# Two transfers instead of six for the gathered heads, weight loads tied to units, and a new order of the first region

## The chip, the cores and the metric

The program runs on one core of one Trainium2 chip, all in float32. The metric is the device time of one execution in microseconds (us). A run's time is that of the whole execution; a profiled execution also has a span, which is the part between its first and last recorded instruction.

## What is computed

Three layers follow each other: a gated linear attention with complex decays, a soft mixture of experts over all tokens, and a mixture that routes each token to one expert. Cut to what matters:

```python
def _attn_ref(q, k, v, a_re, a_im):          # 4 batches, 8 heads, 768 steps, 48 features
    mag = np.sqrt(a_re * a_re + a_im * a_im)
    scale = np.minimum(mag, 0.999) / (mag + 1e-06)
    a_re_n, a_im_n = (a_re * scale, a_im * scale)
    for t in range(S):
        new_re = ar * S_re - ai * S_im       # ar, ai: step t, one value per feature d
        new_im = ar * S_im + ai * S_re
        S_re, S_im = (new_re + k_t v_t^T, new_im)
        y[:, :, t] = q_t^T S_re

def _moe_ref(x, phi, w1, w2):                # x: 3072 x 384, 8 experts, 32 slots
    logits = x @ phi
    slot_input = softmax(logits over tokens).T @ x
    slot_out[e] = relu(slot_input[e] @ w1[e]) @ w2[e]      # 384 x 1024, 1024 x 384
    return softmax(logits over slots) @ slot_out

def _moe2_ref(x, w_gate, w1, w2):            # each token goes to its best of 8 experts
    out[mask] = gate_w * (relu(x[mask] @ w1[e]) @ w2[e])
```

## The kernel before

**Units and groups.** The attention's 3072 tokens are cut into 24 units of 128 steps (4 batches of 6 chunks). One unit holds all 8 heads. Units are taken in 13 groups of one or two; a group's decays `a_re`, `a_im` are loaded together (`decl_A`, L415) and turned into logarithms and angles. For each unit, `decl_B` (L442) loads k, q and v, forms running sums of the logarithms and of the angles with TensorE (L457, a product with a triangular matrix) and multiplies k and q by the exponentials (L466, L467). `decl_C` (L494) makes the features and does the unit's attention.

**Features and the gathered heads.** The features lie on the partitions: tile `F` (L349) has three blocks of 128 partitions. Heads are taken in four pairs. A block holds the 48 features of one head of its pair at partitions 0 to 47 and of the other at 64 to 111. The fourth pair has no block of its own: a third of each of its heads (16 features) sits in the spare partitions 48 to 63 and 112 to 127 of each block. `feature_rows` (L45) lays this out on the host. L505 multiplies k and q by cosine and sine into `F` (VectorE, or GpSimd where the order says so). Then the thirds of the fourth pair have to be brought together: for each of its two heads, three DMAs on SyncE's queue (L509) each move 16 partitions of one block into tile `M`, 16 x 513 floats or 32.1 KB each, six DMAs a unit:

```python
for i in range(2):
    for j in range(3):
        d, o = 64 * i + 16 * j, 64 * i + 48
        dma(32768, lambda j=j, d=d, o=o: nc.sync.dma_start(out=M[d:d + 16, :nx], in_=F[o:o + 16, j, :nx]), ...)
```

**The unit's products.** TensorE transposes the k features (L528; copied to `kT` by L532 and L533, whose second copy puts the gathered pair's features into the same order as `M`), multiplies q features by k features to scores (L543, three head pairs from `F` and the fourth from `M`), forms the k-v products (L563), the part of the output inside the chunk (L581) and the part from the carried state `S` (L590, again with `F` and `M`), and transposes the output (L618). VectorE masks the scores (L552) and updates the state (L605, L607, L609). Every fourth unit, `decl_M` (L628) adds the four units to the soft mixture's logits and to a running softmax over tokens. After the last unit a short closing chain ends with `siT` (L673), the slots' inputs.

**The second region** begins with the soft mixture's experts: first layer L797 with the `w1` weights of 8 experts (four products of 12 matrix steps), transposes L806, second layer L826 with the `w2` weights (four products of 16 steps), then L837 and the routed layer.

**Weights.** Each expert's `w1` and each `w2` is 1536 KB. Eight tiles `wr0` to `wr7` lie beside the first region's tiles and take the eight `w1` (L728). Five tiles `wl0` to `wl4` take the place of the first region's tiles (features, k and q, v, ...) once these are done, and hold `w2` of experts 0 to 4 (L774). The `w2` of experts 5 to 7 go into `wr0` to `wr2` after the first four first-layer weights are used, in halves of 768 KB (L814). All transfers named here are issued by SyncE and stand in its one queue in the order of the program.

**What sets the order.** `Sched.op` (L127) records each operation with its engine, an estimated duration and what it reads and writes. For the first region a table of numbers, `ORDER[0]`, gives a sequence of all operations and which engine does those that have a choice; it is followed word for word (`follow`, L210). `place` (L147) walks that sequence with the estimated durations, `MODE` (L102, the cost of changing from one kind of matrix product to another) and `LAT`; `emit` (L222) writes the instructions in the order of the start times so found. So every engine executes its own fixed list, in order, and the semaphores make it wait where an input is not there. `emit` also puts small unused products (`fill`, L731) into TensorE's gaps near the start. In the sequence of before, five of the eight `w1` loads stand among the units and three after or around the last unit's gather.

Of the kernel before, what the change touches and what calls it, by code (L numbers as in the profile page):

```python
# [44 lines left out]
def feature_rows():  # L45

    f = np.zeros((3, 128), np.int64)
    for j in range(3):
# [21 lines left out]
    "FaQ()7yvW?JODrdH~>WeNB|H3TmVb}U;tzQBme*aPykc_tN^e8v;b%Ui~t+}EC5&lXaH>hZ~zPdkN}hbm;i_Xpa3WUxB#R8r~sS*y#RCocmTuzgaC{I%mBauI2FkN1OY$++yHz4kO7nd>;Uxu_yEKK"  # L70
    "nE{{y1ORLS<N$yG2mwR^odNs+&;ZB*00AHX@BrWd%mHu#r~%Od*#SraOaXKOd;!z|tO3{nv;oxtumN}hfB_f*3<13X-~ojJxB*ZB>;mWk+yUhQ906nj@B)Yd00I;OI0IAx5CIec^Z^J05dsVX^aAJr"
    ">;Y{8ECC<_JOd;G9Rm0P@Bx?t7y=*xBmw*ZC;>156a&BkX##)(SOFLV`2sWnGy*sRcmkmUKm+^&Z~`a-I00M%U;!`!d;**Tqyj7ga037XR0BN$gaSkZNdt5P1Or$DTmyIm90MQ&r~-5XX#*$&tO6th"
    "1OhPw2m@>bd;^37JOWSxOao8@hysBFKmtSpNCHd(U;~H)umZFKR05;{%mfSrECav-!~)0yWCP3s&;m3DGy{<Xj02PdoC93~paYBo5Ci-KqyzK>m;<Z>SOSm&NClJvv;#~9PzAUGxdTlEyaLb!00pQ6"
    "NCeaZWCUCUzyrhs)C5=r+ycA<$O9Aw-~t#0*#sN~R0J#qcmz-c+ypoV%mdg01O*WV2nFB+<O6{OYy=DiU<4!u&;!&1R0VtlgaqIOFa_iU*aL_Jj08Le_yqg|AO)NRumdy|+ym$X>;sSl00bxnbp$vC"
    "lms*dK?UdpJO%IrKnC;!pafV2qy%6E_yg<&Tm|q1Xa%SQtOT$G2n1yX<N|O6cm==&zy-Vo=mKO0Xa-ycYzBY@1q4I|fChvHa0P4y>;?1%@dXS7L<SKA6a+m4d<B>Uc?O&YXatA`7zA(zbOn?KyadDq"
    "NCq4Ppawt$&;`i^bOwwDkOs5_xCXoiqz14CgawEN*ag4_%mw%btOg(i)CG(Mlm+|+$OXg(SOzQv;04SExCCSfkOj~Ns0PRe<ORe9U<OPE=>>cSXb9W|00syKlm{^c1O^xg)CQObm<E^yoCTl-wFaaG"
    "s0G{x6b4WRR0c!{7zTI<qz4=bum_w6*#_tatOaZcL<9^55C*UX90p(lWCA1vAPB4n2nWOm5eI+>BnAuzoCqKWC<cTGj0pS&NC=1sxCaFX<OTo-a0qk=pa@I|Bnb2dC<sspqzEVnya&Mt>;^0cL<h(R"
# [1331 lines left out]
```

## Time and profile before

| what | value |
|---|---|
| median of 3 runs | 320.6 us (319.21 to 322.67) |
| the profiled execution, its own time | 322.03 us |
| its span | 320.0 us |
| mean granted TensorE clock, as a share of full speed | 0.947 |
| TensorE matmul busy | 278.9 us, 87% of the span |
| VectorE busy | 230.3 us, 72% |
| ScalarE busy | 202.1 us, 63% |
| GpSimd busy | 80.1 us, 25% |
| moved by DMA | 62.79 MB, mean 196 GB/s |

The first region ends, and L797 begins, at 235.7 us of the span; the second layer L826 ends at 273.2 us. A matmul's record in float32 counts twice (two passes), so "x16" in a row of TensorE is eight matrix steps. Busy time is an average over stages with different limits, so the stages are read one by one. Idle time of an engine that nobody waits for costs nothing.

### The profile page before, as it was taken

The page shows a single profiled execution, that of the slowest core. Times are in us where ns is not written, and L with a number is a line of the kernel's source. Part 1 is how long each engine was busy: PE and PEld are TensorE (multiplying, and loading weights), DVE is VectorE, ACT ScalarE, POOL GpSimd, SP SyncE. Part 2 cuts the span into 40 slices and gives each one's busy share as a digit, 9 for nine tenths or more (in the row PEclk, how much of TensorE's full clock was granted, in tenths as well). Part 3 has the DMA queues.
Part 4 walks back from the last instruction along what each step waited for, and adds up shares of the span by engine and source line. Part 5 has one row for each costly group of instructions (what it writes and reads, how often), then busy time and mean ns, then how long its engine had stood idle before and what let it go on. Part 6 is the DMA issues. An engine that isn't in the chain of part 4 may idle for free.

```text
span 320.0 us, 9381 instructions
## 1 busy us (share of the span) xinstructions
PE 278.9 (87%) x3764; PEld 220.0 (69%) x3764; DVE 230.3 (72%) x478; ACT 202.1 (63%) x423; POOL 80.1 (25%) x94
## 2 busy tenths in 40 slices
PE   0995989889999998998899898979898597999990
PEld 0884868769878877887778697867642132688970
DVE  2689898799989999986989886866465030558750
ACT  7599598968998898997597766543232010434760
POOL 1016225534433557340452324111000000000000
PEclk9998799999999999997999999999979798967997
DMA  7934366564656345548275535554899993190482
GB/s 243 349 80 147 109 205 190 160 228 140 189 170 193 113 147 165 189 115 311 74 247 188 174 83 169 176 183 141 340 378 373 374 371 136 48 349 1 186 325 88
DMA packets 32323, 62.79 MB, mean 196 GB/s; under 512 B 4128, under 2 KB 19872, under 8 KB 32272
## 3 DMA queue, kind: packets, MB, share of 16 engines
q1 hardware_dynamic: 32272, 62.12, 58.3%
q8 instruction: 31, 0.51, 0.7%
q14 instruction: 20, 0.16, 0.2%
HBM read 52.66 MB, written 4.72 MB: 179 GB/s over the span
## 4 chain that ended last, share of the span: by engine, by line
PE 46%; DVE 11%; DMA 9%; SPq 9%; issue 3%; ACT 1%; DVEq 0%; ACTq 0%
PE bank L543 6%; PE bank L581 5%; PE bank L457 5%; SPq L509 5%; DMA M<-F 5%; PE bank L590 4%; DMA wr<-w 4%; SPq L814 3%; DVE F L505 3%; PE bank L797 3%; PE bank L563 3%; PE bank L528 2%; PE bank L618 2%; PE bank L1121 1%; PE bank L826 1%
## 5 line engine op out<-in xcount | busy, mean ns | idle before, releaser
L457 PE MATMUL bank<-cst,lt 128*128 128x128 f32 x288 | 41.3, 287 | 9.4 <-DMA cst<-cst 8.3
L457 PEld LDWEIGHTS bank<-cst,lt 128*128 128x128 f32 x288 | 36.4, 197 | 11.8 <-ACT lt L435 8.3
L505 DVE TENSOR_TENSOR F<-kqi,lt 128x768 f32<-128x768 f32 x35 | 39.7, 1158 | 3.7 <-PE bank L590 2.7
L543 PE MATMUL bank<-F 48*128 48x128 f32 x576 | 41.1, 284 | 0.4 <-DVE kqi L466 0.3
L543 PEld LDWEIGHTS bank<-F 48*128 48x128 f32 x576 | 36.4, 192 | 5.0 <-issue 1.6
L552 DVE TENSOR_TENSOR sc<-bank,cst 128x512 f32<-128x512 f32 x48 | 31.3, 684 | 10.4 <-PE bank L543 9.9
L733 ACT ACT_TABLE_LOAD x27 | 34.6, 1283 | 1.2 <-PEq L1392 0.7
L581 PE MATMUL bank<-sc,v 128*64 128x128 f32 x384 | 31.9, 292 | 2.6 <-DMA v<-v 1.8
L505 POOL TENSOR_TENSOR F<-kqi,lt 128x768 f32<-128x768 f32 x13 | 24.9, 1925 | 29.2 <-PE bank L590 14.5
L479 POOL TENSOR_TENSOR lt<-lt,n 128x384 f32<-128x384 f32 x15 | 16.7, 1115 | 45.2 <-DVE n L478 39.9
L581 PEld LDWEIGHTS bank<-sc,v 128*64 128x64 f32 x384 | 21.6, 143 | 8.1 <-issue 4.5
L543 PE MATMUL bank<-M 48*128 48x128 f32 x192 | 18.8, 284 | 8.6 <-DMA M<-F 7.2
L590 PE MATMUL bank<-F,St 48*48 48x128 f32 x480 | 25.6, 283 | 0.0
L411 ACT COPY yT<-bank 112x256 f32<-112x256 f32 x39 | 13.6, 373 | 16.4 <-PE bank L590 14.0
L528 PE MATMUL bank<-cst,F 128*128 128x128 f32 x120 | 20.1, 286 | 3.9 <-DVE F L505 2.9
L543 PEld LDWEIGHTS bank<-M 48*128 48x128 f32 x192 | 15.3, 188 | 10.8 <-issue 7.4
L411 ACT COPY kT<-bank 128x288 f32<-128x288 f32 (+1 forms) x63 | 18.6, 328 | 5.8 <-PE bank L528 3.9
L590 PEld LDWEIGHTS bank<-F,St 48*48 48x48 f32 x480 | 16.2, 122 | 6.1 <-issue 5.4
L826 PE MATMUL bank<-wl,hT 128*32 128x384 f32 x80 | 16.0, 601 | 4.3 <-DMA wl<-w 4.3
L563 PE MATMUL bank<-v,kT 128*48 128x48 f32 x640 | 19.7, 210 | 0.0
L563 PEld LDWEIGHTS bank<-v,kT 128*48 128x48 f32 x640 | 17.1, 125 | 3.6 <-issue 2.1
L528 PEld LDWEIGHTS bank<-cst,F 128*128 128x128 f32 x120 | 13.9, 145 | 6.1 <-DVE F L505 2.2
(249 smaller groups left out, 594.7 us busy)
## 6 DMA issues: line engine op xcount, KB each, us to landing
wr<-w SPq DMA_DIRECT2D x8, 1536.0 KB, 8.5
kqi<-kq SPq DMA_DIRECT2D x24, 384.0 KB, 3.6
reim<-reim SPq DMA_DIRECT2D x11, 768.0 KB, 5.2
wl<-w SPq DMA_DIRECT2D x5, 1536.0 KB, 17.2
v<-v SPq DMA_DIRECT2D x24, 192.0 KB, 3.5
wr<-w SPq DMA_DIRECT2D x6, 768.0 KB, 12.2
M<-F SPq DMA_DIRECT2D x120, 32.1 KB, 2.4
out<-osb SPq DMA_DIRECT2D x10, 384.0 KB, 2.4
```

What stands on the lines that cost most here:

```text
L411: v = {"A": ("ACT", t_act(n, True), lambda: nc.scalar.copy(out=out, in_=in_()), False), "D": ("DVE", t_dve(n), lambda: vec.tensor_copy(out ...
L457: pe.matmul(bank(kb)[:, 128 * i:128 * i + 128], lt[:, j, 128 * i:128 * i + 128], (tri, tri2)[j], start=True, stop=True)
L479: either("P", 384, lambda e: e.tensor_tensor(out=lt[:, 1], in0=lt[:, 1], in1=n, op=ALU.subtract), r=[kth, kn], w=[kth])
L505: either(e, 768, lambda e, i=i, b=b: e.tensor_tensor(out=Fv[:, i], in0=kq, in1=b, op=ALU.mult), r=[(kkq, 0), (kkq, 1), klt(u, i)], w=[kF[i]])
L528: pe.transpose(bank(kb)[:, 128 * j:128 * j + 128], F[:, j, 128 * x:128 * x + 128], idn)
L543: pe.matmul(bank(kbs[i])[:, 128 * q:128 * q + 128], kind(q, i, x), kind(q, i, 2 + x), start=(x == 0), stop=(x == 1))
L552: op("DVE", t_dve(512), lambda i=i, msk=msk: vec.tensor_tensor(out=sct[scs[i]], in0=bank(kbs[i]).rearrange("p (h t) -> p h t", h=4), in1=m ...
L563: pe.matmul(kvps[64 * i:64 * i + 48, q, 48 * x:48 * x + 48], w, v[:, 48 * h:48 * h + 48], start=True, stop=True)
L581: pe.matmul(out(q, i, 64), v[:, 48 * h:48 * h + 64], sct[scs[i]][:, q], start=True, stop=(c == 0))
L590: pe.matmul(out(q, i, 48), S[64 * i:64 * i + 48, q, 48 * x:48 * x + 48], kind(q, i, 2 + x), start=False, stop=(x == 1))
L733: tab = lambda t: nc.scalar.preload_act_table_set(TABLES[t])
L826: pe.matmul(bank(kbo)[32 * j:32 * j + 32, :384], hT[2 * q + hf][:, k, 32 * j:32 * j + 32], w2v(4 * q + j)[:, 4 * hf + k], start=(hf == 0 a ...
```

## The change

It has four parts.

1. `feature_rows` gives block j every third feature of the gathered heads (j, j+3, j+6, ...) instead of 16 features in a row. So the three blocks' values of one partition are three features in a row, and one DMA moves a whole head: 16 partitions x 3 blocks of `F` go to 48 partitions of `M`. A unit has two gathers of 96 KB instead of six of 32 KB. `kT`'s second copy writes in the new order.
2. The eight `w1` loads are declared beside units 4, 6, ..., 18, and an empty TensorE operation of units 6, 8, ..., 20 is said to read them, so that a sequence has to place each load before that point. The operation issues nothing, so no engine waits for these loads there.
3. The planner's estimates are changed: a gather is 620 + 2100 ns, a change of product kind always 97 ns, and the products' durations are new.
4. `ORDER[0]` is a new sequence for the first region, with other choices of engine.

```diff
@@ feature_rows
-            f[j, 64 * i + 48:64 * i + 64] = 48 * pair(3)[i] + 16 * j + np.arange(16)
+            f[j, 64 * i + 48:64 * i + 64] = 48 * pair(3)[i] + j + 3 * np.arange(16)
@@ ORDER
...
-MODE = [[0 if i == j else 95 if j else 24 for j in range(5)] for i in range(5)]
-for _i, _j in ((1, 2), (2, 1), (1, 3), (3, 1), (2, 3), (3, 2), (1, 4), (4, 1), (2, 4), (4, 2), (3, 4), (4, 3)):
-    MODE[_i][_j] = 95
+MODE = [[0 if i == j else 97 for j in range(5)] for i in range(5)]
@@ decl_C
         for i in range(2):
-            for j in range(3):
-                d, o = 64 * i + 16 * j, 64 * i + 48
-                dma(32768, lambda j=j, d=d, o=o: nc.sync.dma_start(out=M[d:d + 16, :nx], in_=F[o:o + 16, j, :nx]), r=kF + kX, w=[("M", u % NF, i, j)])
+            d, o = 64 * i, 64 * i + 48
+            op("SP", 620, lambda d=d, o=o: nc.sync.dma_start(out=M[d:d + 48, :nx], in_=F[o:o + 16, :, :nx]), r=kF + kX, w=[("M", u % NF, i)], lat=2100)
...
-                copy("D", 96, kTt[b][:, 288:].rearrange("p (i j r) -> p j i r", j=3, i=2), lambda kv4=kv4: kv4()[:, :, :, 48:], r=[kb], w=[("kT", b, 1)])
+                copy("D", 96, kTt[b][:, 288:].rearrange("p (i r j) -> p j i r", j=3, i=2), lambda kv4=kv4: kv4()[:, :, :, 48:], r=[kb], w=[("kT", b, 1)])
...
-        op("PE", 2, lambda: None, r=kF, w=[kbs[0]], acq=kbs[0], mode=2)
-        op("PE", 870, SC((0, 1)), r=kF, w=kbs, acq=kbs[1], mode=2)
-        op("PE", 870, SC((2, 3)), r=kF + kM, w=kbs, mode=2)
+        kwt = [("w", u // 2 - 3)] if 6 <= u < 6 + 2 * NWR and u % 2 == 0 else []
+        op("PE", 2, lambda: None, r=kF + kwt, w=[kbs[0]], acq=kbs[0], mode=2)
+        op("PE", 893, SC((0, 1)), r=kF, w=kbs, acq=kbs[1], mode=2)
+        op("PE", 893, SC((2, 3)), r=kF + kM, w=kbs, mode=2)
...
@@ the loop over groups
         for u in us:
             decl_B(u)
+            if u % 2 == 0 and 4 <= u < 4 + 2 * NWR:
+                i = u // 2 - 2
+                dma(1572864, lambda i=i: load_w(wr[i], *w_src[i]), w=[("w", i)])
...
-    for i in range(NWR):
-        dma(1572864, lambda i=i: load_w(wr[i], *w_src[i]), w=[("w", i)])
```

What the new sequence does is seen in the lists of the engines. The first place is SyncE's queue at the end of the first region. `M` from `F` is a gather, `wr` from `w1` a first-layer weight load, `wl` from `w2` a second-layer load. Before:

```order
L448 DMA kqi1_105<-kq 128x768
L449 DMA v3_109<-v 128x384
L389 DMA wr4_81<-w1 128x3x1024
L509 DMA M1_113<-F1_111 16x512 x6
L389 DMA wr6_83<-w1 128x3x1024
L389 DMA wr1_78<-w1 128x3x1024
L389 DMA wl0_2912<-w2 128x8x384
L389 DMA wl1_2913<-w2 128x8x384
```

The same place in the changed kernel (its lines are three lower):

```order
L505 DMA M0_112<-F0_110 48x1x513 x2
L445 DMA kqi1_105<-kq 128x768
L505 DMA M1_113<-F1_111 48x1x512 x2
L446 DMA v3_109<-v 128x384
L386 DMA wl0_2825<-w2 128x8x384
L386 DMA wl1_2826<-w2 128x8x384
```

The three `w1` loads around the last gather are gone from here; `wl0` follows the last unit's gathers and its v. The eighth `w1` load now stands before the gathers of the third unit from the end.

The second place is SyncE's queue in the middle of the first region, around a `w1` load. `reim` is a group's decays, `kqi` and `v` the inputs of one unit. Before:

```order
L449 DMA v0_106<-v 128x384
L389 DMA wr0_77<-w1 128x3x1024
L428 DMA reim1_97<-reim 128x2x768
L509 DMA M1_113<-F1_111 16x513 x6
L509 DMA M0_112<-F0_110 16x513 x2
```

And in the changed kernel, around another such load:

```order
L386 DMA wr5_82<-w1 128x3x1024
L425 DMA reim0_98<-reim 128x2x768
L445 DMA kqi1_105<-kq 128x768
L446 DMA v1_107<-v 128x384
L505 DMA M1_113<-F1_111 48x1x513 x2
L505 DMA M0_112<-F0_110 48x1x513 x2
L445 DMA kqi0_104<-kq 128x768
```

One load more stands before the first units' inputs, at the start of the program, and six stand among the units, mostly with a `reim` load right behind.

The third place is TensorE's list from the last unit's output to the last product that makes `siT`. The names are: `x` with `dd` the softmax-weighted tokens, `yT` with `phiI` the last unit's logits, `ex` and `ltc` transposes of exponentials and logits, `stw` with `acc` and `dd` with `x_129` the sums that make `siT`. Before:

```order
L681 MATMUL bank_75<-x_126,dd 32x384
L681 MATMUL bank_75<-x_127,dd 32x384
L681 MATMUL bank_75<-x_128,dd 32x384
L700 MATMUL bank_74<-cst,row 128x1
L637 MATMUL bank_71<-yT_124,phiI 128x128 x4
L690 MATMUL bank_70<-cst,ltc 128x128
L618 MATMUL bank_72<-cst,yT_124 128x112 x4
L706 MATMUL bank_74<-mx,cst 128x1
L690 MATMUL bank_69<-cst,ltc 128x96
L665 MATMUL bank_71<-cst,ex 128x32
L662 MATMUL bank_73<-stw,acc 128x32 x3
L670 MATMUL bank_73<-dd,x_129 128x32 x3
```

And in the changed kernel:

```order
L615 MATMUL bank_72<-cst,yT_121 128x112 x4
L634 MATMUL bank_74<-yT_124,phiI 128x128 x4
L678 MATMUL bank_75<-x_126,dd 32x384
L678 MATMUL bank_75<-x_127,dd 32x384
L678 MATMUL bank_75<-x_128,dd 32x384
L703 MATMUL bank_69<-mx,cst 128x1
L662 MATMUL bank_74<-cst,ex 128x32
L687 MATMUL bank_73<-cst,ltc 128x96
L615 MATMUL bank_70<-cst,yT_124 128x112 x4
L687 MATMUL bank_74<-cst,ltc 128x32
L659 MATMUL bank_71<-stw,acc 128x32 x3
L667 MATMUL bank_71<-dd,x_129 128x32 x3
```

The last unit's logits now stand ahead of the weighted-token products instead of behind them; the number of products up to `siT` is nearly the same.

Counted over the whole first region in the two lists: TensorE changes from one kind of product to another 142 times before and 133 times now. VectorE makes 33 of the 48 feature products instead of 35 (GpSimd 15 instead of 13) and 10 of the 20 subtractions of L479 instead of 5. ScalarE has two more table loads. The table of numbers itself is not shown.

## Rows read from the trace of the kernel before

**Rows 1.** The profile's page: busy time, and the DMA share in 40 slices.

```profile
PE 278.9 (87%) x3764; PEld 220.0 (69%) x3764; DVE 230.3 (72%) x478; ACT 202.1 (63%) x423; POOL 80.1 (25%) x94
...
DMA  7934366564656345548275535554899993190482
```

**Rows 2.** Stretches: from:to, length, busy of each engine, granted clock, DMA share, GB/s.

```profile
20.00:230.00 210.00, 192.97 (x3153) 162.95 (x3154) 178.71 (x343) 160.12 (x340) 77.86 (x80) 0.98 0.55 172
...
235.00:247.00 12.00, 11.78 (x87) 3.58 (x86) 7.91 (x12) 3.56 (x6) 0.00 (x0) 0.87 1.06 373
247.00:269.00 22.00, 16.07 (x132) 5.39 (x136) 3.06 (x8) 1.09 (x4) 0.00 (x0) 0.92 0.96 337
...
273.20:320.00 46.80, 37.76 (x262) 32.75 (x260) 26.79 (x80) 20.95 (x45) 0.64 (x1) 0.85 0.47 171
```

**Rows 3.** The chain that ended last, end of the second layer: start, length, what.

```profile
235.67 6.56 PE bank L797 x48
...
256.92 11.79 DMA wr<-w
268.75 4.47 PE bank L826 x28
```

**Rows 4.** Timeline of TensorE, first and second layer: start, length, instruction, [idle before].

```profile
242.16 0.66 PE L806 MATMUL bank<-cst,hid 128*128 128x128 f32 x4
242.75 2.78 PE L797 MATMUL bank<-wr,siT 128*32 128x512 f32 x24
...
251.98 4.36 PE L826 MATMUL bank<-wl,hT 128*32 128x384 f32 x26 [3.39 <-DMA wl<-w]
...
259.45 2.76 PE L826 MATMUL bank<-wl,hT 128*32 128x384 f32 x32
```

**Rows 5.** Timeline of SyncE's queue, 212 to 244 us: start, length of the issue.

```profile
212.33 0.43 SPq L389 DMA_DIRECT2D wr<-w  x1
218.50 3.71 SPq L509 DMA_DIRECT2D M<-F  x6
222.25 2.10 SPq L389 DMA_DIRECT2D wr<-w  x2
224.45 19.51 SPq L389 DMA_DIRECT2D wl<-w  x5
```

**Rows 6.** What TensorE waited for, 20 to 235 us: total us, times, longest.

```profile
PE bank L543 <- DMA M<-F: 7.2, 7, 2.2
PE bank L528 <- DVE F L505: 2.9, 3, 1.2
```

**Rows 7.** The gather's line L509: issue in ns (least, median, most); landing.

```profile
L509 SPq DMA_DIRECT2D M<-F x144: 507/587/1973, 19.4 to 221.6; - x144
...
DMA to landing us min/median/max: 1.9/2.3/5.5
```

**Rows 8.** DMA issues: count, KB each, median us to landing.

```profile
v<-v SPq DMA_DIRECT2D x24, 192.0 KB, 3.5
...
reim<-reim SPq DMA_DIRECT2D x2, 192.0 KB, 2.5
```

**Rows 9.** The chain in the middle: one and two runs of the same product.

```profile
95.00 0.58 PE bank L590 x16
...
96.96 1.02 PE bank L590 x32
```

**Rows 10.** Timeline of TensorE at the first unit's gather, columns as in rows 4.

```profile
27.24 0.81 PE L543 MATMUL bank<-M 48*128 48x128 f32 x8 [2.21 <-DMA M<-F]
```

**Rows 11.** One stretch of 6 us behind that, columns as in rows 2.

```profile
30.00:36.00 6.00, 5.12 (x32) 3.94 (x33) 6.00 (x8) 3.96 (x8) 2.04 (x2) 0.50 0.12 27
```

**Rows 12.** Costly groups of the page that the change moves.

```profile
L505 DVE TENSOR_TENSOR F<-kqi,lt 128x768 f32<-128x768 f32 x35 | 39.7, 1158 | 3.7 <-PE bank L590 2.7
...
L733 ACT ACT_TABLE_LOAD x27 | 34.6, 1283 | 1.2 <-PEq L1392 0.7
```

**Rows 13.** Copies into kT by engine and shape, ns.

```profile
L411 ACT COPY kT<-bank x63: 217/387/424, 20.6 to 217.9; 128x288 f32<-128x288 f32 x34, 128x96 f32<-128x96 f32 x29
```

More of the change, by code (lines that the diff above doesn't have):

```diff
@@ L69 @@
 ORDER = [
[L70 to L77, printed above, removed]
@@ new lines @@
+    "Gy&`Yv;p7%U;#J*i2;lOxB)!@ya7M~WC3UazyWXplmVCl^Z=XzQ~}Tc_yGI>00F!L8~}9z1OW&GTmftWcmc=(kO9R33<KBz%mEMq)dA1}*Z~j&6ay3i7y&>7^Z}#+-~pfk00Kk-Bmt-aAOWobNC5}|"
+    "3<3B7Ndim){Q*n?zyeSK83V)uumLCmL<8sn>;c>X1Of;GTmta{EdlHT$O0q-AOr9M<O1{p903#pU;<?V3<CH9=mJOsC<815OamAK5CSj)%mQ=*cmg>C0RtQZFasO{AOhq8Py+k{R0C83d;-t{SOPQx"
+    "XaZ3KI0!rgSOX*iC;}`3fC5|tgaVKP1OtEsGy{|Zm;#&v-~ylm)B<G#`~+wNa03wp*aB?=tOBtDZ~}M(00o2ts03^SI0A?Qgam;Di~@}Vd;{D9%moYt6a=IKJpu#;$OPa7%mj!8jRY(Nhy&0Bv;w#S"
+    "<OHw;v;>d@xCD>`7z6|W)C9l;yaeb3qywk}*aVaVm;=NF2?aO=JOn@lbOV$Gm;}%TU;~^3paZM}r~<$PL<H0Y*affyv;(*UNCZ>_SOn|@oCGig3<VSg5Cyyg%meTQ!~<LeU<70Ypahf$9Rwf+^aRKQ"
@@ new lines @@
+    "`2-yW`~`FbGz35bqy!)Ya0Ji;00smGXay(*C<OEcB?Q$2WCcV57zQ*390uG4cm#a}gauFrm<Qkmcm*H^B?b`&6b4KLfCYR7C<agjhy{%W2nHktR0f;}*aPGRECnnEkOf!<Fa<OPYy~(5Kn7?8+yq<("
+    "pa<LoYy><8a0QeFm<4nNJO$_lqy_K=WCmddYzAlstOPIyI0YC5L<S57patv&Km|kvs09E7Nd}|`s0T;|Oa)K{Bng}aSOwq%B?sUK_yyz##0MA%xCM9y<O5U%tOc+Iv<1Kgyakj7od)m&bp`|k=m+%!"
+    "?FUT;Tm_g0hz5`bKnExZ2n3A=@CSef_yfoX%m-ivv<A2aNe4s+AO|!D90>daAPB4nd<HlNga*6^BnbQm*ay%CJO|JRpa!G{um`jUOb4h2C<m|xtOhIx)CVjH)CTki00=1va0XBZR0l8#U<bSgzy<^e"
+    "EC{FyFbKp3Tn7;dWCvIWXa{Tu$Og;?2naL@Gzb+4a0j>t3<z`wcn5q3pb6XtI0--q_y^bqga=#*U<il@JqS<;=mS^?R0zZc$pusiSP3u(un52hObMh3tO{ia-3L$!JPEW2;0CY?KnX|)gbC#aL<nFB"
@@ new lines @@
+    "Yzc4)bP2c!s0ru>6bD2JXb5ZwTnT6iWC`2|tO;-k>;`lQ;0U}3<Op~OObB=hd<lpNj0uDYkO`Ctd<cLDhzLjtfCsb+j0o@skO-6runD*cm<YfK><F|8&<N-Vpa`4@xC)pF#0bm^^a{lZr3mx}I1Km*"
+    "{0IOE*a*A|1PKTU_zL_A6bZozoCz2Q>;w1)j0eaG)CkQ8EDHe(L<&F(&<fZJ1P43}$p~NykOvqE1Pd?=5DUx+2nX;8+zQ|dGz&ls90$M(<O+ZZ^ayDR><TywKnn~B5DCNz&<Ows)Cpw@Yzh<$7z@}5"
+    "ND4g*ObT!cbPC`J{02k}+zAK^=nCWs=n3oz@CqCYNDN2|@Coz@{0YbkgbYLrcnS;)ybM(fR0>!MT?%{(ObciXhzyJjQ43HC01hAv3<vlL2nuWr5C?D!Obi4LBnyxXlnluW#0$U-hzbk}fC`KXkP4X!"
+    "5DF9u7z$tvgbI8NlnOKoC<|~4WDB4SbPUuAcnqiroC;73SPN(i019mj1q!VQ90^nmBnlx32o8J;fD6P7$qdj8%?w-%SPbwBgbRoZ3=Yr>^b5=j_zR2+c?*~fkPDa#bPJRVoC~B3oD6^rpbG#D{0j^W"
@@ L381, in build @@
     for i, t in enumerate(Mt):
-        op("POOL", 600, lambda t=t: pool.memset(t, 0.0), w=[("M", i, j, k) for j in range(2) for k in range(3)])
+        op("POOL", 600, lambda t=t: pool.memset(t, 0.0), w=[("M", i, j) for j in range(2)])
     op("DVE", 600, lambda: vec.memset(banks[7], 0.0), w=[("kv", 0), ("kv", 1)])
@@ L498, in decl_C @@
         F, M = Ft[u % NF], Mt[u % NF]
-        kF, kM = [("F", u % NF, i) for i in range(2)], [("M", u % NF, i, j) for i in range(2) for j in range(3)]
+        kF, kM = [("F", u % NF, i) for i in range(2)], [("M", u % NF, i) for i in range(2)]
         kX = [("F", u % NF, 2)] if c < NC - 1 else []
```

35 lines of the change are left out of this document (15 added, 20 removed).

## The prediction

> **What bounds the kernel now.** I read the page first, then the chain that ended last, then the stretches between the places that the chain names, and last the waits and SyncE's queue.
>
> The page shows TensorE with matmuls for 87% of the span and VectorE for 72% [rows 1]. That hides two stages with different limits. In the DMA line of the slices the last third has a run of nines: there the 16 DMA engines never rest. The table of stretches says when: from 235 to 247 us the DMA share is 1.06 at 373 GB/s, from 247 to 269 it is 0.96, and 0.47 behind that [rows 2]. In the same time the chain waits 11.79 us for a weight load, up to 268.75 us, and TensorE has 4.47 us of second layer left behind it [rows 3]. So the first two expert layers are bound by the weights. In the first region, 20 to 230 us, TensorE is busy 193.0 of 210 us and VectorE 178.7, with DMA at 0.55 [rows 2]: it is bound by TensorE's list and the waits in it, with VectorE close behind. Most of the listed waits are for the gathers: 7.2 us in seven pieces, the longest 2.2 us; 2.9 us go to features that VectorE has not finished [rows 6].
>
> **Part 1: the w1 loads leave the tail.** A w1 or w2 load is 1536 KB, 1.573 MB, so 4.2 us at 373 GB/s [rows 2]; a half takes 2.1 us. SyncE issues one of the last three w1 loads at 212.33 us, which flies before the last gathers, and two more from 222.25 us, then five w2 loads [rows 5], and six halves follow (L814). From 222.25 these are 7 x 4.2 + 6 x 2.1 = 42.0 us of transfers, and the last lands at 268.75 [rows 3], 46.5 us later: 4.5 us go to the start, the landing and small pauses. The tail is thus one queue from the last gather to the last half, and nearly always full.
>
> In the changed list no w1 load stands here, so 33.6 us of transfers remain. With the first region unchanged, the last unit's first gather is issued at 218.50 [rows 5]; two gathers at 0.59 us [rows 7] and one more issue put the first w2 load at about 220.3. The last half lands at 220.3 + 33.6 + 4.5 = 258.4. The halves go into tiles that the first two products of the first layer read, and those end at 235.67 + 6.56 = 242.2 [rows 3]; the five w2 loads keep the queue full until about then, 220.3 + 2 + 21.0 = 243.3 (2 us until bytes flow, as a gather's least landing is 1.9 [rows 7]), so the halves find no gap.
>
> What is late next is TensorE: two first-layer products 6.56 us [rows 3], two more at about 2.7, four groups of transposes at 0.6, four second-layer products at 2.7 (the printed lengths hold some 0.06 of overlap) [rows 4]. That is 25.2 us, and 235.67 + 25.2 = 260.9. The last of these products would start at 258.2, so the last half at 258.4 and TensorE's list come out together, at 261.1. The second layer now ends at 268.75 + 4.47 = 273.2 [rows 3]. **Gain 12.1 us**, of which 8.4 are the two loads, 1.9 the earlier start and 1.8 a last product at full pace. TensorE's list allows 12.3 at most. Below, it is 8 us if the w2 loads flow some 4 us later than I think, since two of their tiles lie where the last unit's features are still read. Behind 273.2 us nothing is changed: 46.8 us stay [rows 2]. TensorE's clock is 0.85 of full there, and the shorter pause ahead may shift that by some 2 us either way.
>
> **Part 2: two gathers instead of six.** An issue of a gather takes 0.587 us in the median [rows 7]; the last unit's six took 3.71 us in all [rows 5]. Two take 1.2, so a head is complete 2.4 us sooner, if its landing does not grow. The new size, 96 KB, lies between 32 KB at 2.3 us [rows 7] and 192 KB at 2.5 us on a calm queue, 3.5 us in the v loads among other traffic [rows 8]; I take 2.5, nearest in kind to the calm one. That is 2.2 us net a unit, as long as the longest of the waits. With all seven gone, the gain is 7.2; with none, because features then come late, it is 0. I take **6 us**, since SyncE's queue also passes k, q and v sooner and the next lateness, VectorE's features, is 2.9 us now [rows 6].
>
> The Trainium skill speaks against this part: DMA: Bandwidth & Descriptors, section "Issuing engines are not separate DMA queues", holds that the time a sequencer needs to start a DMA is usually small beside the DMA itself. This trace disagrees for the gathers, with 3.71 us of issues beside a landing of 2.3; by the page this part would be worth nothing, which is the first rival below.
>
> **Part 3: the order.** One run of a product of sixteen records takes 0.58 us and two runs joined 1.02 [rows 9], so a change of kind costs about 2 x 0.58 - 1.02 = 0.14 us. Nine changes fewer are worth **1.3 us**. VectorE gives up two feature products at 1.158 us [rows 12] and takes five subtractions of half that size: between 2.3 us less and 3.5 us more (if a subtraction cost as much as a feature product); I take nothing. Two more table loads of 1.283 us [rows 12] fall on ScalarE, which is idle 50 of 210 us [rows 2]: nothing, at most 2.6 us. The kT copies with a stride of three: 40 copies of 96 values, the quickest 0.217 us [rows 13]. ScalarE and VectorE make them; I take nothing; if each took twice as long, it were 40 x 0.22 = 8.8 us over both engines, and some 3 of it on the path if, as now, VectorE made about a third. The closing list from the last output to siT holds nearly the same products; moving the last logits ahead there can shift its end by about one such product, 0.6 us [rows 4], and I take nothing.
>
> Near the start TensorE waits 2.21 us for the first unit's gather [rows 10], and behind that, from 30 to 36 us, its granted clock is 0.50, the lower level of 1.2 GHz [rows 11]. In those 6 us VectorE is fully busy, so only part counts: at half rate 6 us hold at most 3 us of loss, and I take back **1 us**.
>
> **Part 4: more loads in the first region.** The two loads taken out of the tail bring 8.4 us of transfers into a stretch whose DMA share is 0.55 [rows 2]. The cost is nothing if they fall in pauses and cannot exceed 8.4. It is 6.4 us if each holds up a gather as long as the worst one seen, 5.5 against 2.3 us in the median [rows 7]. With six loads there now, all of TensorE's waits for gathers sum to 7.2 us [rows 6], about 1.2 a load; I take **2 us** of loss.
>
> **The sum.** -12.1 - 6 - 1.3 - 1 + 2 = -18.4 us. The profiled execution took 322.0 us (span 320.0 and 2.0 around it), so 303.6. It lay 1.4 above the median of the three runs, 320.6, and against that median I predict 302.2 us. About 1% is what a measurement of this kernel can tell from no change.
>
> **The rivals.**
>
> *The gathers are hidden anyway.* VectorE's features are late instead, and parts 2 and the clock give nothing: 322.0 - 12.1 - 1.3 + 2 - 1.4 = 309.2. For it speaks that VectorE is busy 85% of the first region [rows 2]; against it, the seven waits on TensorE itself. Chance 0.2.
>
> *The first region closes up much more.* TensorE is idle 17 of its 210 us [rows 2]; with 11 of these gone, 3 from the clock and no loss to the loads, 322.0 - 12.1 - 11 - 3 - 1.3 - 1.4 = 293.2. For it: the sequence is made anew as a whole. Against it: some waits are each other's shadow. Chance 0.12.
>
> *Slower: loads in front of gathers.* In the new list six w1 loads stand among the units, mostly with a 768 KB reim load behind them: 4.2 + 2.1 = 6.3 us of queue that a gather right behind has to sit out. Without part 4 the gains are 20.4 us; so it decides from 20.4 / 6.3, more than three places with the full wait, and four cost 25.2: 322.0 + 4.8 - 1.4 = 325.4. For it: two of the loads come from a place where the queue was in nobody's way. Against it: six loads already run there and no gather took over 5.5 us [rows 7]. Chance 0.06.
>
> *The large gather is slow.* If it lands in 5.5 us, the worst of the small ones, the unit's gather ends 0.8 us later than now; seven times that is 5.6 of loss for 6 of gain, 302.2 + 11.6 = 313.8. Chance 0.06.
>
> *The w2 loads do not start sooner.* If they all waited for the end of the first region at 235.7, the last half would land at 235.7 + 33.6 + 4.5 = 273.8, 5.0 us later than now: part 1 becomes a loss of 5.0, and the time 302.2 + 17.1 = 319.3, the same as before within 1%. Against it: the first of them is issued at 224.45 now [rows 5], with the region still running. Chance 0.06.
>
> **How the numbers follow.** My forecast has 0.5. Faster by over 1% (under 317.4) are it, the first two rivals and the slow gather: 0.88. The late w2 loads count as within 1%, 0.06; the queue in front of the gathers as slower, 0.06. The range 293 to 314 leaves out the last two, and half of the closing-up and slow-gather cases; the bounds of parts 1 to 4 (0 to 7 for the gathers, 8 to 12.6 for the tail, 0 to 8.4 for the loads) lie mostly within it.
>
> **What would show it.** Right: 48 gathers of 96 KB landing in 2.3 to 3 us; TensorE's wait for M at 1 to 2 us; the last w1 load landed before the last unit's gathers; the DMA's full stretch about 33 us long; the second layer some 25 us after its start and without a wait of over 1 us; L797 starting at 225 to 231 us. Wrong in part 1: L826 still waiting for a weight load at its end. Wrong in part 2: VectorE's features in place of M at the head of TensorE's waits. The forecast as a whole fails if L797 starts later than at 235.7 us.

## The result, and the profile after

The changed kernel takes 296.4 us in the median of four runs (292.7 to 299.3); the kernel before, beside it, 321.6 (319.2 to 323.6). The ratio is 0.914, with a 95% interval of 0.901 to 0.927. Measured once more, again with the kernel before beside it, it is 0.923 (0.910 to 0.937). The profiled execution took 294.8 us. The ratios of this document leave disturbed runs out, so they can differ by two per cent from the quotient of the medians.

The forecast was 302.2 us, with a range of 293 to 314. The time is 5.8 us below the forecast and inside the range.

The page of the kernel after, which answers to [rows 1]: busy time, then the granted clock and the DMA share in 40 slices.

```profile
PE 264.8 (90%) x3778; PEld 215.1 (73%) x3778; DVE 226.7 (77%) x486; ACT 203.3 (69%) x418; POOL 88.9 (30%) x93
...
PEclk9999999999999999999999999999999999958997
...
DMA  7926796969679736979553747050999990750782
```

The clock's line shows one dip only, far behind the experts. The long run of nines in the DMA line is shorter than before.

The next rows are stretches, with the columns of [rows 2]. First the kernel before, from 20 us to the start of the experts, and its two expert layers:

```profile
20.00:235.67 215.67, 197.94 (x3189) 166.94 (x3187) 182.23 (x359) 162.28 (x350) 77.86 (x80) 0.97 0.56 178
235.67:273.20 37.53, 31.49 (x241) 9.83 (x241) 10.71 (x19) 4.58 (x10) 0.00 (x0) 0.88 0.88 311
```

The same two stretches of the kernel after, and the rest of it:

```profile
20.00:218.57 198.57, 190.20 (x3204) 163.32 (x3202) 180.70 (x371) 162.89 (x345) 84.12 (x79) 1.00 0.68 210
218.57:246.00 27.43, 25.39 (x241) 8.92 (x241) 9.69 (x18) 4.47 (x9) 0.00 (x0) 1.00 0.87 305
246.00:292.90 46.90, 37.75 (x260) 32.76 (x260) 26.78 (x80) 20.97 (x45) 0.64 (x1) 0.86 0.47 170
```

The span is 27.1 us shorter: 17.1 in the first region, 10.1 in the two layers, nothing behind them (46.9 against 46.8 in [rows 2]). Each gain can be split with the second number of a row, TensorE's busy time. In the first region TensorE is idle 8.4 us instead of 17.7, and busy 190.2 instead of 197.9. So 9.4 us are waits that went. The other 7.7 are busy time of nearly the same work, with a granted clock of 1.00 where it was 0.97. The clock is not all of it: a kernel with the old order, further below, is busy 192.1 us at the same 0.97. In the layers the waits fell from 6.0 to 2.0 us, and the busy time from 31.5 to 25.4 with the clock up from 0.88 to 1.00.

What TensorE waited for from 20 to 212 us, as [rows 6]; then the line of the gather, as [rows 7]:

```profile
PE bank L560 <- DVE kT L408: 1.0, 1, 1.0
PE bank L615 <- DVE kqi L463: 1.0, 1, 1.0
PE bank L524 <- DVE F L502: 1.0, 2, 0.7
PE bank L587 <- POOL St L606: 0.9, 1, 0.9
PE bank L539 <- DMA M<-F: 0.9, 2, 0.7
```

```profile
L505 SPq DMA_DIRECT2D M<-F x48: 567/578/826, 19.2 to 203.8; - x48
...
DMA to landing us min/median/max: 2.6/2.9/5.6
```

No engine stands out among these waits any more. A gather of 96 KB lands in 2.9 us, 0.6 later than one of 32 KB, and its issue is as long as a small one's.

The end of SyncE's queue in the first region, and behind it, as [rows 5]:

```profile
203.22 1.21 SPq L505 DMA_DIRECT2D M<-F  x2
204.47 0.58 SPq L446 DMA_DIRECT2D v<-v  x1
205.16 13.29 SPq L386 DMA_DIRECT2D wl<-w  x5
222.24 11.13 SPq L812 DMA_DIRECT2D wr<-w  x6
```

TensorE's timeline where the layers start and where they still wait, as [rows 4]:

```profile
218.57 5.36 PE L795 MATMUL bank<-wr,siT 128*32 128x512 f32 x48 [0.33 <-ACT siT L408]
...
241.16 0.83 PE L824 MATMUL bank<-wr,hT 128*32 128x384 f32 x2 [0.83 <-DMA wr<-w]
243.21 0.52 PE L824 MATMUL bank<-wr,hT 128*32 128x384 f32 x2 [1.21 <-DMA wr<-w]
```

The five `w2` loads follow the last gathers, with no `w1` load between. From the first of them, 205.16 + 33.6 + 4.5 = 243.3 us; the last half is waited for until 243.21. The queue arithmetic of part 1 thus holds to 0.1 us. TensorE starts the layers 13.4 us behind the first `w2` load, where I had 235.7 - 220.3 = 15.4. These 2.0 us less of a lead are the 0.83 + 1.21 us of waits that are left.

### The profile page after: what moved, and what is told of

It is laid out like the page before. It is cut to its first block, busy times and chain, and to the rows that moved or that the text cites. A ratio compares the mean times of both kernels' runs of the same rounds, so it can differ in the third digit from the quotient of the medians.

```text
span 292.9 us, 9220 instructions
## 1 busy us (share of the span) xinstructions
PE 264.8 (90%) x3778; PEld 215.1 (73%) x3778; DVE 226.7 (77%) x486; ACT 203.3 (69%) x418; POOL 88.9 (30%) x93
## 4 chain that ended last, share of the span: by engine, by line
PE 52%; DMA 14%; DVE 12%; ACT 8%; issue 4%; POOL 4%; SPq 2%; DVEq 0%; POOLq 0%; ACTq 0%
PE bank L539 9%; DMA kqi<-kq 6%; PE bank L578 5%; PE bank L587 5%; PE bank L454 5%; DMA wr<-w 4%; DVE F L502 4%; PE bank L560 3%; PE bank L795 3%; PE bank L524 3%; POOL F L502 2%; PE bank L615 2%; DMA reim<-reim 2%; PE bank L729 2%; DMA M<-F 2%
## 5 line engine op out<-in xcount | busy, mean ns | idle before, releaser
L502 POOL TENSOR_TENSOR F<-kqi,lt 128x768 f32<-128x768 f32 x15 | 34.1, 2281 | 30.6 <-PE bank L587 20.8
L539 PE MATMUL bank<-F 48*128 48x128 f32 x576 | 39.3, 278 | 0.6 <-DVE kqi L463 0.6
L502 DVE TENSOR_TENSOR F<-kqi,lt 128x768 f32<-128x768 f32 x33 | 35.5, 1106 | 1.5 <-ACT lt L488 1.3
L578 PE MATMUL bank<-sc,v 128*64 128x128 f32 x384 | 29.7, 281 | 0.5 <-DVE sc L549 0.5
L578 PEld LDWEIGHTS bank<-sc,v 128*64 128x64 f32 x384 | 20.4, 136 | 5.7 <-issue 3.7
L428 POOL TENSOR_TENSOR lt<-reim,lt 128x768 f32<-128x768 f32 (+1 forms) x10 | 17.9, 1790 | 19.8 <-ACT lt L427 19.8
L524 PE MATMUL bank<-cst,F 128*128 128x128 f32 x120 | 18.9, 279 | 1.7 <-DVE F L502 1.0
L606 POOL TENSOR_TENSOR St<-Ut,Dt 112x384 f32<-112x384 f32 x15 | 13.1, 873 | 23.9 <-DVE Ut L604 13.3
L476 POOL TENSOR_TENSOR lt<-lt,n 128x384 f32<-128x384 f32 x10 | 12.9, 1287 | 20.1 <-DVE n L475 17.4
L539 PE MATMUL bank<-M 48*128 48x128 f32 x192 | 16.5, 276 | 0.9 <-DMA M<-F 0.9
```

The source lines that it names most:

```text
L428: either("P", n, lambda e: e.tensor_tensor(out=l1, in0=im, in1=l0, op=ALU.mult), r=[kim] + k0, w=k1)
L502: either(e, 768, lambda e, i=i, b=b: e.tensor_tensor(out=Fv[:, i], in0=kq, in1=b, op=ALU.mult), r=[(kkq, 0), (kkq, 1), klt(u, i)], w=[kF[i]])
L524: pe.transpose(bank(kb)[:, 128 * j:128 * j + 128], F[:, j, 128 * x:128 * x + 128], idn)
L539: pe.matmul(bank(kbs[i])[:, 128 * q:128 * q + 128], kind(q, i, x), kind(q, i, 2 + x), start=(x == 0), stop=(x == 1))
L578: pe.matmul(out(q, i, 64), v[:, 48 * h:48 * h + 64], sct[scs[i]][:, q], start=True, stop=(c == 0))
L606: either("P", 384, lambda e: e.tensor_tensor(out=S1, in0=Ut, in1=dcy, op=ALU.mult), r=["U"] + kD, w=[kS1])
```

## The experiments

All kernels keep the lists of their parent, engine by engine, except for the edit named. "Old lists" are those of the kernel before, "new lists" those of the kernel after. They ran on three chips, and a ratio is to the kernel before on the same chip. The region's end is the start of the experts' first layer in the profiled execution; those of the two gathers alone and of the loads alone came out 6.7 and 3.5 us above their own medians, so for these two the times and ratios count more than the profile.

| kernel | median us | ratio to before | region's end | layers us |
|---|---|---|---|---|
| before | 320 to 323 | 1 | 235.7 | 37.5 |
| two gathers, old lists | 300.5 | 0.933 (0.925 to 0.942) | 224.0 | 34.4 |
| loads moved, old lists | 316.6 | 0.970 (0.961 to 0.978) | 241.7 | 28.7 |
| both, old lists | 295.8 | 0.926 (0.914 to 0.938) | 222.5 | 26.6 |
| after | 296.4; 295.0 | 0.914; 0.923 | 218.6; 218.7 | 27.4; 27.9 |
| after, six gathers | 334.5 | 1.044 (1.037 to 1.051) | 255.9 | 28.6 |
| after, loads in the tail | 301.5 | 0.937 (0.928 to 0.946) | 217.1 | 34.9 |

### One part at a time

**Two gathers in the old lists.** The kernel before, with the layout in triples and two DMAs a unit; of the six places in each engine's list, a head's first remains.

```diff
-            for j in range(3):
-                d, o = 64 * i + 16 * j, 64 * i + 48
-                dma(32768, lambda j=j, d=d, o=o: nc.sync.dma_start(out=M[d:d + 16, :nx], in_=F[o:o + 16, j, :nx]), r=kF + kX, w=[("M", u % NF, i, j)])
+            d, o = 64 * i, 64 * i + 48
+            op("SP", 620, lambda d=d, o=o: nc.sync.dma_start(out=M[d:d + 48, :nx], in_=F[o:o + 16, :, :nx]), r=kF + kX, w=[("M", u % NF, i)], lat=2100)
```

> The kernel before with one edit: two gathers of 96 KB a unit in place of six of 32 KB, and the features in triples. TensorE, VectorE, ScalarE and GpSimd run the old lists instruction for instruction, and the w1 loads stay where they were. If the issue time of the gathers is what the first region waits for, its end (235.7 us) comes 5 to 7 us sooner and the time is 314 to 316 us against 321. If the new order is what counts and the gathers are hidden, the region's end moves by under 1.5 us and the time is 319 to 322.

Measured: 0.933, which is 21 us of 320. The gathers alone are worth more than three times the 6 us of part 2, and both expectations missed. The region up to the experts and the two layers, with the columns of the stretches above:

```profile
20.00:224.00 204.00, 193.64 (x3184) 165.11 (x3183) 181.60 (x358) 161.60 (x350) 79.36 (x80) 0.96 0.62 191
224.00:258.37 34.37, 27.86 (x241) 9.05 (x241) 10.70 (x19) 4.59 (x10) 0.00 (x0) 0.96 0.91 321
```

This execution's span, 305.1 us, is 14.9 us shorter than that of the kernel before. TensorE's idle time in the region falls by 7.4 us (10.4 against 17.7), its busy time by 4.3, though the clock is no higher, and the layers take 3.2 us less.

**The loads in the old lists.** Only the sequence is changed: the last three `w1` loads stand ahead of the decay loads of groups 8, 9 and 10.

```diff
@@ SyncE's list, without line numbers
...
 DMA kqi<-kq 128x768
+DMA wr<-w 128x3x1024
 DMA reim<-reim 128x2x768
...
 DMA v<-v 128x384
-DMA wr<-w 128x3x1024
 DMA M<-F 16x512 x6
-DMA wr<-w 128x3x1024
-DMA wr<-w 128x3x1024
 DMA wl<-w 128x8x384
```

The three added rows stand each ahead of such a decay load; one is shown.

> The kernel before with one edit: the last three w1 loads stand in front of three reim loads in the middle of the first region instead of around the last gather; six gathers and the old lists on all other engines. If the weight queue sets the end of the second layer, L826 ends 25.5 to 28 us after L797 starts instead of 37.5, and the time falls by 8 to 12 us, to 309 to 313, with the first region up to 2 us longer. If loads in front of gathers cost what they save, the first region gets 6 us longer or more and the time is 315 or above.

Measured: 0.970, or 9.7 us (6.9 to 12.4), but this rests on the two quickest of the runs. All ten lie from 308.6 to 320.9 us, and their median is 3.4 us below that of the kernel before. I had worked out 12.1 for the tail less 2 for the crowded region, 10.1 together. In the profiled execution (320.1 us) the layers take 8.8 us less, and the region ends 6.0 us later, as the second expectation has it. One wait there is as long. First SyncE's queue, then TensorE's timeline:

```profile
130.00 0.58 SPq L388 DMA_DIRECT2D wr<-w  x1
130.69 0.42 SPq L427 DMA_DIRECT2D reim<-reim  x1
131.16 0.47 SPq L448 DMA_DIRECT2D v<-v  x1
```

```profile
141.10 0.88 PE L562 MATMUL bank<-v,kT 128*48 128x48 f32 x16 [6.06 <-DMA v<-v]
```

A v load stands behind a `w1` load and a decay load, lands 9.9 us after its issue, and TensorE waits 6.06 us for it. So with six gathers the crowded region can cost what the tail saves; whether the quicker runs are without this wait is not on record.

**Six gathers in the new lists.** The first edit's diff with + and - exchanged, in the kernel after; the six DMAs stand where the two stood.

> The changed kernel with one edit undone: six gathers of 32 KB a unit, each former gather as three in a row at the same place of SyncE's queue; new lists on the other engines. If the gathers' issue time counts in the new order too, the first region gets 6 to 10 us longer and the time is 302 to 306 against 296. If the new order alone made the region shorter, the time stays at 295 to 298.

Measured: 334.5 us, far beyond both expectations; 12 to 13% of the time before are lost against the kernel after. This is a kernel with the loads moved and the new order, yet it is slower than the kernel before: the new lists do not bear six gathers. Its first region, with the columns of the stretches above, then two rows of what its engines waited for (total, times, longest):

```profile
20.00:255.92 235.92, 213.02 (x3197) 181.57 (x3195) 181.22 (x371) 162.78 (x345) 78.34 (x79) 0.91 0.54 175
```

```profile
DVE kqi L463 <- DMA kqi<-kq: 18.7, 7, 4.7
...
PE bank L540 <- DMA M<-F: 13.7, 14, 2.3
```

Against the kernel after, the region is 37.4 us longer: 14.5 us more idle, 22.8 us more busy, with the clock at 0.91 instead of 1.00. The waits name M for 13.7 us only; VectorE waits 18.7 us for k and q, which stand in the same queue.

**The loads back in the tail, new lists.** The kernel after with its last three `w1` loads around and behind the last gathers.

```diff
-        kwt = [("w", u // 2 - 3)] if 6 <= u < 6 + 2 * NWR and u % 2 == 0 else []
+        kwt = []
```

SyncE's list has the three `wr<-w` rows then where the `-` rows of the loads' diff stand.

> The changed kernel with one edit undone: the last three w1 loads stand again around and behind the last unit's gathers; two gathers and the new lists elsewhere. If the tail is one full queue, two loads of 4.2 us more put the last half 8.4 us later and the time is 303 to 305 against 296, with a first region as long as or 1 to 2 us shorter than that of the changed kernel. If TensorE's list sets the tail instead, the time rises by under 3 us.

Measured: 0.937 against 0.914 and 0.923. By the medians that is 5 us more than the kernel after, between the two expectations. The layers take 34.9 us instead of 27.4, the region ends 1.5 us earlier. So the move takes 7.5 us out of the layers here and gives 1.5 back in the region; in the old lists with two gathers it takes 7.7 out of them (34.4 to 26.6).

**Both edits in the old lists.** The first two edits together: all of the change but its new lists.

> The kernel before with its own lists, the two 96 KB gathers a unit, and the last three w1 loads moved ahead into the first region: all of the change but its new lists. Theory A (the gathers carry most of the gain, the new lists add little when gathers are cheap): the two single edits gave 19.5 and 3.4 us from 320, so together 297, plus or minus 3, and the changed kernel's lists are worth 0 to 3 us on top of it. Theory B (the new lists are worth much by themselves, as the 38 us between six and two gathers in the new lists could suggest): this stays at 301 or above and the lists bring 5 us or more.

Measured: 0.926, against 0.914 and 0.923 for the whole change. The intervals overlap: the new lists are worth 0.3 to 1.2%, not told apart from nothing by these runs, and no 5 us, as theory A has it. In the profiles the region ends 3.9 us earlier with them. One thing that they do change is the clock near the start: from 20 to 60 us, in the kernel with both edits and old lists,

```profile
20.00:60.00 40.00, 36.38 (x500) 31.57 (x499) 36.10 (x62) 34.12 (x73) 17.22 (x18) 0.87 0.61 172
```

and in the kernel after:

```profile
20.00:60.00 40.00, 37.67 (x588) 32.20 (x586) 37.24 (x69) 36.55 (x73) 18.22 (x20) 1.00 0.76 240
```

So this dip was not the doing of the six gathers, as I had thought from [rows 10] and [rows 11]: it stays with two gathers in the old lists and is gone with the new. With six gathers in the new lists the clock of this stretch is 0.96.

### What of the six gathers costs the time

Two theories were left. By the first, a head that is complete late costs the time (TensorE waits for M). By the second, SyncE's queue does, since everything behind the six issues comes later. To tell them apart, four small DMAs a unit were put behind the two large gathers. The head is then complete as early as in the kernel after, and SyncE issues as many DMAs as before. Their data is read by nobody.

**DMAs of 8 KB, into four tiles used in turn, old lists and new lists.**

```diff
+    dmy = [at.tile([16, 128], F32, name=f"dmy{i}") for i in range(4)]
...
+            for j in range(1, 3):
+                dma(8192, lambda x=2 * i + j - 1: nc.sync.dma_start(out=dmy[x], in_=a["cst"][:16, :128]), w=[("dmy", 2 * i + j - 1)])
```

> The kernel before with two 96 KB gathers a unit, and behind a unit's second gather four DMAs of 8 KB into tiles that nobody reads: SyncE issues as many DMAs as before, but a head is complete as early as with two gathers alone. Theory L (what the six gathers cost is that a head is complete late: TensorE waits for M, and falls from its clock's upper level): the time stays near that of the two gathers alone, 300.5, within 4 us. Theory Q (what they cost is SyncE's queue: 0.587 us an issue, and k, q and v loads and the next unit's gathers stand behind them): the gain is lost for the most part, 312 us or more.

> The changed kernel with four DMAs of 8 KB, two behind each gather of a unit, put behind the unit's second gather, into tiles that nobody reads. With six gathers in place of two these lists took 334.5 us, 38 more. Theory L (a head that is complete late costs it): 296 to 302. Theory Q (the queue costs it): 320 or more, since SyncE's queue is as long as with six gathers.

Measured: 328.9 us in the old lists (323.7 to 330.9), 324.7 in the new (313.6 to 329.2; ratio 0.999, 0.988 to 1.010). In the old lists the edit brought a wait of its own: a small DMA waits for the one that wrote the same tile a unit before.

```profile
SPq L510 <- DMA dmy<-cst: 14.3, 9, 3.1
```

So this kernel can't carry the verdict, and both were repeated without that wait.

**DMAs of 512 bytes, each into a place of its own.**

```diff
+    dmy = at.tile([16, 32 * NU], F32, name="dmy")
...
+                dma(512, lambda u=u, x=2 * i + j - 1: nc.sync.dma_start(out=dmy[:, 32 * u + 8 * x:32 * u + 8 * x + 8], in_=a["cst"][:16, :8]), w=[("dmy", 2 * i + j - 1, u)])
```

> The kernel before with two 96 KB gathers a unit and, behind a unit's second gather, four DMAs of 512 bytes, each into a place of its own that nobody reads, so that none of them has to wait for an older one (the DMAs of 8 KB shared four tiles, and SyncE waited 14.3 us for them). SyncE issues as many DMAs as before the change, and a head is complete as early as with two gathers alone. Theory Q (SyncE's queue is what six gathers cost): 312 us or more, near the kernel before. Theory L (a head that is complete late is what they cost): 297 to 305, and the 329 us of the 8 KB version came from its extra wait.

> The changed kernel with the same four DMAs of 512 bytes a unit, each into a place of its own. Theory Q: 313 to 330, as with the four DMAs of 8 KB. Theory L, or if the bytes and the shared tiles of those were the cost: 296 to 302.

Measured: 315.1 us, ratio 0.986 (0.979 to 0.993) in the old lists; 322.7 us, ratio 1.017 (1.010 to 1.025) in the new. Both are what theory Q expected. Of what two gathers gain, (0.986 - 0.933) / (1 - 0.933) = 0.79 is lost again in the old lists, and in the new (1.017 - 0.914) / (1.044 - 0.914) = 0.79. The intervals of the ratios leave about 0.7 to 0.9. The new lists' five runs lie from 315.7 to 324.2 us, and by the two quickest alone the share is 0.6. So most of the cost, about four fifths, comes with the four more issues; the rest is left for the late head, and for what the small DMAs do not copy of the six: four of them hold the queue for 2.0 us in the rows below, four gathers for some 2.4. What the small DMAs move is hardly the cost. The packets of the queue, in the kernel with 512-byte DMAs and in the kernel after (new lists; packets, MB, time as a share of the 16 DMA engines' span):

```profile
q1 hardware_dynamic: 33808, 62.17, 61.4%
```

```profile
q1 hardware_dynamic: 30736, 62.12, 65.4%
```

That is 192.6 us of 313.7 against 191.6 of 292.9, 1.0 us more.

In the new lists the trace, taken of a run 7.0 us below its median, names what the queue makes late: VectorE's wait for k and q, and TensorE's for M, in the kernel with 512-byte DMAs,

```profile
DVE kqi L464 <- DMA kqi<-kq: 14.2, 11, 4.5
...
PE bank L542 <- DMA M<-F: 1.8, 3, 1.4
```

and in the kernel after:

```profile
DVE kqi L463 <- DMA kqi<-kq: 3.7, 5, 1.2
```

M is hardly waited for in either. Here is a pair of units in that queue:

```profile
65.93 0.58 SPq L506 DMA_DIRECT2D M<-F  x1
66.56 2.06 SPq L508 DMA_DIRECT2D dmy<-cst  x4
68.74 1.02 SPq L446 DMA_DIRECT2D kqi<-kq  x1
69.86 0.58 SPq L506 DMA_DIRECT2D M<-F  x1
...
71.15 0.57 SPq L506 DMA_DIRECT2D M<-F  x1
71.78 1.96 SPq L508 DMA_DIRECT2D dmy<-cst  x4
73.79 0.90 SPq L447 DMA_DIRECT2D v<-v  x2
```

Behind the first unit's small DMAs stand the next load of k and q and the second unit's gathers, each some 2 us late. For the old lists the times show the same share, but no single wait carries it. Between the profiles of the two gathers alone and of the two gathers with 512-byte DMAs the region grows by 12.0 us. Of these 2.2 are idle time of TensorE and 9.8 busy time (203.4 us against 193.6), with the clock at 0.93 instead of 0.96. Why the clock fell there stays open. Whether gathers issued from another engine's queue would cost less was not tried.

### A version that might beat both

In the kernel after, the last half of `w2` is still late by 2.0 us. So half of the first `w2` load (768 KB) was moved ahead of the last three units, into the tile of a decay buffer that is done by then.

```diff
+    dma(786432, lambda: nc.sync.dma_start(out=rek, in_=a["w2"][0, :512].rearrange("(k p) f -> p k f", p=128)), w=[("re", 1), ("im", 1)])
...
-                        pe.matmul(bank(kbo)[32 * j:32 * j + 32, :384], hT[2 * q + hf][:, k, 32 * j:32 * j + 32], w2v(4 * q + j)[:, 4 * hf + k],
+                        pe.matmul(bank(kbo)[32 * j:32 * j + 32, :384], hT[2 * q + hf][:, k, 32 * j:32 * j + 32], (w2v(4 * q + j)[:, 4 * hf + k] if q + j + hf else rek[:, k]),
```

> The changed kernel with half of the first w2 load (768 KB, 2.1 us at 373 GB/s) moved from the queue of the second layers ahead of the last three units, into the tile of a reim buffer that is done by then. In the changed kernel the last half of w2 still lands last, and TensorE waits 0.83 and 1.21 us for it. Expected if the queue bounds these layers: the last half lands about 2 us sooner and the time falls by 1.5 to 2.5 us, to about 294.5. If TensorE's own list bounds them instead, or the early load holds up the last gathers: no change, or 1 to 2 us more.

> The changed kernel once more, for a comparison on one chip with the version that has half of a w2 load in the first region: 293 to 299 us, as measured first.

> The changed kernel with half of the first w2 load moved into the first region, once more, beside the changed kernel on the same chip. If the first measurement, 290.95 us, holds: 289.5 to 293 and 3 to 5 us below the changed kernel. If part of that was the chip: 1.5 to 2.5 us below it, as the queue's arithmetic gives.

Measured: first 291.0 us (289.9 to 292.3; ratio 0.907, 0.897 to 0.917), then, beside the kernel after on one chip, 293.1 against 295.0 (ratios 0.920 and 0.923). By the medians that is 1.9 us less, as the queue's arithmetic gives, but well within the intervals: a gain is not shown. The profiles say why it is small: the layers take 24.9 us in both runs, just TensorE's list, but the region ends 2.1 and 3.5 us later. What the half load saved in the layers was lost in the first region. Of the waits for the last halves this is left, in TensorE's timeline of the second run:

```profile
244.40 0.52 PE L827 MATMUL bank<-wr,hT 128*32 128x384 f32 x2 [0.37 <-DMA wr<-w]
```

## Why the prediction was right, and where it was off

**The forecast and its direction: right.** The range held, and of the signs named for it these came: 48 gathers, landing in 2.9 us; TensorE's wait for M at 0.9 us (I had said 1 to 2); the last `w1` load issued at 165.8 us, long before the last gathers. Others did not. The layers take 27.4 us and not some 25, with a wait of 1.21 us where I had none over 1, and so the sign of being wrong in part 1 came: the second layer still waits for a weight load at its end, 2.0 us in all. The sign of being wrong in part 2, VectorE's features at the head of TensorE's waits, came in part: with 1.0 us they stand level with two others. The experts start at 218.6 us, where I had 225 to 231. The sum was 18.4 us, the profile shows 27.1.

**That the range held is partly luck.** Two errors cancel. With part 2 at the 21 us that it measures and the other terms as they stood, the sum is 33.4 us and the time 287.2, outside the range. But the terms do not add: once there are two gathers, the loads give 2 to 7 us instead of 10.1.

**Part 1, the loads out of the tail: right in kind, 2 us too large in the profile.** The queue's arithmetic was exact and TensorE's list is 25.4 us against my 25.2. The term was 12.1 and the layers gave 10.1, since the region closed up faster than the queue's start moved ahead; so the weight queue, and not TensorE's list, still sets their end. Taken alone, parts 1 and 4 together measure 9.7 us for 10.1 by the two quickest runs and 3.4 by the medians. With two gathers in place the old lists show 2.4 us by the ratios (0.926 against 0.933, not told apart from nothing), the new ones 4 to 7.

**Part 2, two gathers for six: the term that was mis-sized.** I took 6 us, bounded by 7.2, the sum of TensorE's waits put down to M [rows 6]. It measures 21 us in the old lists. As a bound on idle time 7.2 was good: the profile of the gathers alone has 7.4 us less of it in the region. What I put at nothing was the rest, in that profile 4.3 us of busy time and 3.2 us in the layers (their first `w2` load is issued 13.1 us ahead of them instead of 11.2); some 6 us more stand between this execution and the median, and no trace shows them. Two things were not in the row. First, it holds one engine's waits for one transfer. The queue is in front of every load: the rows of SyncE's issues from 20 to 205 us sum to 129 us for 189 DMAs before, and to 70 for 111 after. About four fifths of the cost come with the issues, as the small DMAs show. I had named this ("SyncE's queue also passes k, q and v sooner"), but gave it no term of its own: it only served to stay near the bound of 7.2. Secondly, the row holds idle time only, and 7.7 of the region's 17.1 us are busy time. The page had a better view, the chain's shares by line, where SyncE's issues of the gather and their transfers have 5% each, some 30 us together. The page of the kernel before, then of the kernel after:

```profile
PE 46%; DVE 11%; DMA 9%; SPq 9%; issue 3%; ACT 1%; DVEq 0%; ACTq 0%
PE bank L543 6%; PE bank L581 5%; PE bank L457 5%; SPq L509 5%; DMA M<-F 5%; PE bank L590 4%; DMA wr<-w 4%; SPq L814 3%; DVE F L505 3%; PE bank L797 3%; PE bank L563 3%; PE bank L528 2%; PE bank L618 2%; PE bank L1121 1%; PE bank L826 1%
```

```profile
PE 52%; DMA 14%; DVE 12%; ACT 8%; issue 4%; POOL 4%; SPq 2%; DVEq 0%; POOLq 0%; ACTq 0%
```

SyncE falls from 9% of the chain to 2%. Two thirds of the issues gone from that 5% would have been 10 us by themselves, beyond my bound. This is hindsight: shares of a chain are no measured gains.

**The issue time.** The Trainium skill (DMA: Bandwidth & Descriptors, section "Issuing engines are not separate DMA queues") holds that starting a DMA usually takes little beside the DMA itself. Of a single gather that is not refuted: an issue takes 0.58 us beside a landing of 2.9. The prediction set six issues against one landing, which is not what that sentence of the Trainium skill compares. What the runs show is that issues of one queue add up: four more of 512 bytes a unit, with hardly a byte to move, take back 0.6 to 0.9 of the gain.

**Part 3, the order: not refuted, and for another reason.** I took 1.3 us for it and 1 for the clock near the start. The lists measure 0.3 to 1.2% on top of the other parts, 1 to 4 us, not told apart from nothing. The dip of the clock went with the lists and not with the gather. What I did not see is that they suit two gathers only: with six and the loads moved they cost 6 to 7% (334.5 us against 316.6, ratios 1.044 against 0.970), with two nothing.

**Part 4, more loads in the region:** 2 us expected, 1.5 by the two profiles with the new lists. The slower rival, a load in front of a gather, did not come in the changed kernel. With six gathers in the old lists something like it did, in the profile whose region ends 6.0 us later: not a gather but a v load stood behind a `w1` load. Against this rival I had looked at the landings of gathers alone.

**The rivals.** *The gathers are hidden anyway* is refuted by the 21 us. *The region closes up much more*, with 11 of the 17 idle us gone and 3 from the clock, at 293.2 us, was nearest to what happened: 9.4 us of idle time went, and 7.7 of busy time. *The large gather is slow* is refuted by its landing in 2.9 us. *The w2 loads do not start sooner* is refuted by the first one's issue at 205.16 us, 13.4 us ahead of the region's end.

## What to carry to other kernels

Before a cost is bounded by one engine's waits for one transfer, read the chain's shares by line: issues on a shared queue delay every load behind them, and the engines that wait then name those loads, not the culprit (here VectorE's 14.2 us for k and q, in the new lists). Here two terms that work on one queue did not add. Count the issues of a busy queue, and merge transfers by choosing a layout in which one DMA covers them. A fixed order is laid for the costs it was planned with: the same lists that lost nothing with two gathers lost 6 to 7% with six.
